# An attention stage ahead of two feed-forward stages, on one core: two-input products for scalings on VectorE, scalings shared out anew among three engines, shorter keep-warm products, and a new hand-set order with deeper rings

## The chip, the core and the metric

The kernel runs on one core of one Trainium2 chip. The metric is the device time of one execution in microseconds. Five engines of the core work side by side, each through its own queue, in the order in which the program was written: TensorE (PE; its weight loads are listed apart as PEld), VectorE (DVE), ScalarE (ACT), GpSimd (POOL) and SyncE (SP, which here only issues DMAs). An instruction that waits for another engine holds up all that stands behind it on its own engine.

## The reference

Two batches, twelve heads each, 448 positions, 64 channels per head: causal attention, then a gated feed-forward (768 to 1536 to 768) and a second one with a squared ReLU (768 to 2048 to 768). All data are float32 (the weights reach the chip as 64-bit numbers).

```python
scores = (1 / sqrt(64)) * q @ k.T            # 24 heads, 448 x 448
scores = where(above the diagonal, -1e9, scores)
attn = exp(scores - max(scores));  attn = attn / (sum(attn) + 1e-9)
x = (attn @ v), heads side by side           # 896 x 768
x = (silu(x @ w_gate) * (x @ w_val)) @ w_out
out = relu(x @ w_in2)**2 @ w_out2
```

## The kernel before

The twelve pairs of heads (p = 0 to 11; heads 2p and 2p+1) go through attention; each of the feed-forward products is made of three TensorE products of a high and a low part (`whi`, `wlo`, `ahi`, `alo`). A weight unit (128 x 768) is loaded as raw words (`wraw`) and split into `whi` and `wlo` by nine steps, J0 to J8, two on ScalarE and seven on VectorE. 68 units are split in all. Units 0 and 1 are split during attention, and unit 0 is multiplied with the first batch's result there too ("early", six steps G).

The steps of a pair, by the letters of the plan:

- LD loads q, k and v (SP). AT transposes q or k on TensorE into a bank (`qk`), AC copies it to SBUF (tile `qk`).
- S makes the scores of both heads in four row blocks i = 3, 0, 2, 1, with 448, 64, 320 and 192 columns (`s`).
- M (VectorE) scales, masks and takes the extreme value of a row, E (ScalarE) takes the exponential and its row sum, RA adds 1e-9 to four sums at a time (`guard`, tile `st`, 128x4), R is their reciprocal (VectorE).
- N scales a block of the probabilities (tile `P`) by the reciprocal: 448, 256, 192 and 64 columns; NT scales the remaining 64x64 corner. `scale_by` does both: letter D is VectorE, P is GpSimd, A is ScalarE.
- T transposes the probabilities on TensorE in two groups (`pt`): T(h, 0) waits for NT and for blocks 1 to 3 of N. H copies them to SBUF. V multiplies with v (`x`). XH copies the result (`ahi`), XL makes the rest (`alo`).

`attention_plan` lists each step with its engine, a cost, what it waits for and which ring slots it takes; `Plan.run` is a list scheduler that picks at each point the step that can start first, by rank among equals, with the table FIRST added to the ranks. The kernel is then written out in that order, so each engine's queue is fixed when the program is built. Rings set how far a step may run ahead: 8 PSUM banks, 3 raw q and k tiles (`raw`), 4 split tiles (`sp`), 6 probability tiles (`P`). While TensorE would idle in the first 24 us of the plan, `keep_warm` writes products of a constant into the next bank, each 512 columns wide.

Of the kernel before, what the change touches and what calls it, by code (L numbers as in the profile page):

```python
# [16 lines left out]
ALU = mybir.AluOpType  # L17
# [72 lines left out]
    "rings": {'bank': 8, 'raw': 3, 'rawv': 5, 'sp': 4, 'P': 6, 'pt': 4, 'wraw': 3, 'wa': 2, 'wr': 1, 'ws': 3},  # L90
    "ld0": ((1170, 2400), (520, 2450), (1050, 1900), (1050, 1950)),
    "at0": 750,
    "acd": (),
# [5 lines left out]
    "rad": (),  # L99
    "pack": 2,  # L100
    "j": (),
    "xh": (),
# [3 lines left out]
        (0, 0): 'D', (0, 1): 'D', (0, 2): 'D', (0, 3): 'D', (1, 0): 'D', (1, 1): 'D', (1, 2): 'D',  # L106
        (1, 3): 'D', (17, 2): 'D', (21, 2): 'D',
    },
    "h": {
        (17, 1): 0,  # L110
    },
    "nt": {
       
# [26 lines left out]
class Plan:  # L140
# [18 lines left out]
    def run(self):  # L159
# [16 lines left out]
        while ready:  # L176
# [19 lines left out]
            if engine == "PE":  # L196
                now = SHAPE.get(k[0])
                if shape != now:
                    cost += SWITCH[now] + 50 * (now == "columns" and not shape)
                    shape = now  # L200
                cost = warmth.run(start, cost, cols)
            free[engine] = end[k] = start + cost
            if k[0] == "J" and engine == "DVE" and k[2] in (3, 6, 7, 8):
                free["Pool"] = max(free.get("Pool", 0), start) + cost
# [26 lines left out]
def scaling(engine, n):  # L231
    return {"D": ("DVE", 135 + 0.51 * n), "P": ("Pool", max(395, 245 + 0.83 * n)),
            "A": ("ACT", 310 + 0.45 * n)}[engine]


def attention_plan(NP, NPAIR, NC, S, U, KD, rank=RANK, opt=OPT):
# [4 lines left out]
    for p in range(NP):  # L241
# [9 lines left out]
        for z in range(2):  # L251
            sp, bk = ("sp", p), ("bank", "a", p, z)
            add(("AT", p, z), "PE", 390 if p else opt["at0"], [("LD", p, z)] + ([("AT", p, 0)] if z else []), [bk] if z else [bk, sp], [raw, sp] if z else [raw], t + rank["AT"] + z / 2, cols=S * 7 / 8)
            add(("AC", p, z), *(("DVE", dve_cost(S)) if (p, z) in opt["acd"] else ("ACT", act_cost(S))), [("AT", p, z)], [], [sp, bk], t + rank["AC"] + z / 2)
# [11 lines left out]
        for h in (t, t + 1):  # L266
# [18 lines left out]
            add(("NT", h), *scaling(opt["nt"].get(h, "D"), 64), [("R", h), ("N", h, 1)], [], [P],  # L285
# [68 lines left out]
def tile_attention_moe_moe(ctx, tc, q, k, v, w_gate, w_val, w_out, w_in2, w_out2, out):  # L354
# [34 lines left out]
    def keep_warm(ps, n):  # L389
        ones = nc.const_aps.tensor(1.0, [128, 512], BF16)  # L390
        for _ in range(n):
            nc.tensor.matmul(out=ps, lhsT=ones[:, :128], rhs=ones, start=True, stop=True)
# [277 lines left out]
    def scale_by(engine, o, a, by):  # L670
        if engine == "A":
            nc.scalar.activation(out=o, in_=a, func=AF.Copy, scale=by)
        else:
# [3 lines left out]
    def normalise_tail(h):  # L677
        p, at = p_t[h], POFF[2] + 256

        scale_by(OPT["nt"].get(h, "D"), p[:64, POFF[1] + 128:POFF[1] + 192],  # L680
# [115 lines left out]
    with tc.manual_schedule():  # L796
        keep_warm(bank("idle"), 7)
        emit_consts()
        emit_fixed()
        free = 4000  # L800
# [172 lines left out]
```

## Time and profile before

| | us |
|---|---|
| runs shown: 597.0, 597.17, 596.03; median | 597.0 |
| the profiled execution's own time | 596.45 |
| its span in the trace | 594.7 |
| PE busy in the span | 582.0 (98%) |
| DVE busy | 471.4 (79%) |
| ACT busy | 280.9 (47%) |
| POOL busy | 52.5 (9%), all of it in the first 98 us |

The span is 1.75 us shorter than the execution's own time. The page's chain of the work that ended last gives 89% of the span to PE and 7% to DVE. The shares are means over stages with different limits: attention takes about the first 103 us, the feed-forward stages the rest, and POOL works in the first part alone.

### The profile page before, as it was taken

To read this page: it belongs to the slowest core of one execution; us is meant where nothing else is said; L and a number is where in the kernel's file an instruction comes from. 1 tells how busy PE (TensorE), PEld (TensorE's weight loads), DVE (VectorE), ACT (ScalarE), POOL (GpSimd) and SP (SyncE) were. 2 spreads that over 40 slices of the span, in tenths; PEclk is the share of its full clock that TensorE was granted. 3 is DMA by queue.
4 is the path that set the end of the run, shared out by engine and by line. 5 is a ranking of instruction groups with operands and counts; after the bars stand their busy time and mean duration, and the time that the engine had idled before them with its cause. 6 is when DMAs were issued, how large, how long until landed. Compare 5 with 4: busy or idle time off the path is not lost.

```text
span 594.7 us, 8720 instructions
## 1 busy us (share of the span) xinstructions
PE 582.0 (98%) x3232; PEld 531.1 (89%) x3232; DVE 471.4 (79%) x865; ACT 280.9 (47%) x532; POOL 52.5 (9%) x136
## 2 busy tenths in 40 slices
PE   9989899999999999999999999999999999999997
PEld 5756667999999999999999999999999999999997
DVE  2989987898888888888777776888888897649741
ACT  4988885443333333333333224677667733223201
POOL 2364664000000000000000000000000000000000
PEclk9999999999999999999999999999999999999999
DMA  8664231233333333333333333333333344345202
GB/s 170 146 180 104 54 122 55 94 118 106 107 107 106 107 106 109 116 117 121 114 116 107 107 107 106 107 106 107 106 107 107 106 120 147 106 147 145 69 1 93
DMA packets 80778, 65.05 MB, mean 109 GB/s; under 512 B 34912, under 2 KB 76640, under 8 KB 80736
## 3 DMA queue, kind: packets, MB, share of 16 engines
q1 hardware_dynamic: 79808, 64.27, 36.3%
q8 instruction: 25, 0.41, 0.3%
q10 hardware_dynamic: 928, 0.23, 0.2%
q14 instruction: 17, 0.14, 0.1%
HBM read 61.73 MB, written 2.75 MB: 108 GB/s over the span
## 4 chain that ended last, share of the span: by engine, by line
PE 89%; DVE 7%; issue 1%; POOL 1%; DMA 1%; SPq 0%; ACT 0%; ACTq 0%; POOLq 0%
PE o L923 20%; PE h L746 19%; PE v L746 15%; PE y L746 15%; PE g L746 14%; DVE P L642 3%; PE x L718 2%; PE s L624 2%; DVE P L674 2%; PE pt L696 1%; POOL P L674 1%; DMA raw<-in_k_dram 1%; PE early L746 1%; DVE pt L709 1%; PE qk L601 0%
## 5 line engine op out<-in xcount | busy, mean ns | idle before, releaser
L475 ACT ACTIVATE whi<-wa 128x768 fp32r<-128x768 f32 x68 | 57.4, 844 | 123.5 <-DVE wa L469 81.0
L923 PE MATMUL o<-whi,b 128*128 128x384 f32 x336 | 85.6, 334 | 0.0
L746 PE MATMUL y<-b,whi 128*128 128x480 f32 (+1 forms) x288 | 69.2, 362 | 0.0
L457 ACT ACTIVATE wa<-wraw 128x768 f32<-128x768 f32 x68 | 61.8, 909 | 11.4 <-DVE wlo L488 11.1
L746 PE MATMUL h<-b,whi 128*128 128x480 f32 (+1 forms) x256 | 66.7, 362 | 0.0
L485 DVE TENSOR_TENSOR wa<-wa,whi 128x768 f32<-128x768 f32 x68 | 64.7, 952 | 0.4 <-ACT whi L475 0.4
L482 DVE SCALAR_TENSOR_TENSOR wr<-wraw,wr 128x768 f32<-128x768 uint32 x68 | 64.8, 953 | 0.1
L488 DVE TENSOR_TENSOR wlo<-wa,wr 128x768 fp32r<-128x768 f32 x68 | 64.6, 950 | 0.2
L469 DVE SCALAR_TENSOR_TENSOR wa<-wraw,wa 128x768 uint32<-128x768 uint32 x68 | 64.6, 950 | 0.1
L460 DVE TENSOR_SCALAR wa<-wa 128x768 f32<-128x768 f32 x68 | 38.1, 561 | 32.7 <-ACT wa L457 32.7
L923 PEld LDWEIGHTS o<-whi,b 128*128 128x128 f32 x336 | 60.8, 188 | 0.0
L746 PEld LDWEIGHTS y<-b,whi 128*128 128x128 f32 x288 | 54.0, 187 | 3.6
L923 PE MATMUL o<-wlo,b 128*128 128x384 f32 x168 | 56.1, 334 | 0.0
L746 PE MATMUL h<-b,wlo 128*128 128x480 f32 x192 | 53.9, 362 | 0.0
L746 PEld LDWEIGHTS h<-b,whi 128*128 128x128 f32 x256 | 48.0, 187 | 3.2
L648 ACT ACTIVATE P<-P,st 128x320 f32<-128x320 f32 (+3 forms) x84 | 43.9, 528 | 9.5 <-DVE st L642 8.6
L642 DVE CUSTOM_DVE_ANT_0 P<-s,mask 128x448 f32<-128x448 f32 (+3 forms) x96 | 36.6, 414 | 13.3 <-issue 9.7
L833 ACT ACTIVATE b<-u 128x480 fp32r<-128x480 f32 (+2 forms) x24 | 13.9, 580 | 69.4 <-DVE u L829 69.4
L674 POOL TENSOR_SCALAR P<-P,st 128x448 f32<-128x448 f32 (+3 forms) x86 | 41.2, 494 | 18.4 <-DVE st L658 11.4
L746 PE MATMUL v<-ahi,whi 128*128 128x480 f32 (+2 forms) x144 | 40.5, 362 | 0.0
L746 PE MATMUL v<-ahi,wlo 128*128 128x480 f32 (+2 forms) x144 | 40.5, 362 | 0.0
L746 PE MATMUL v<-alo,whi 128*128 128x480 f32 (+2 forms) x144 | 40.5, 362 | 0.0
(89 smaller groups left out, 1053.4 us busy)
## 6 DMA issues: line engine op xcount, KB each, us to landing
wraw<-in_moe_w_out_dram SPq DMA_DIRECT2D x28, 768.0 KB, 4.3
wraw<-in_moe_w_in_dram SPq DMA_DIRECT2D x16, 768.0 KB, 4.7
wraw<-in_moe_w_gate_dram SPq DMA_DIRECT2D x12, 768.0 KB, 4.3
wraw<-in_moe_w_val_dram SPq DMA_DIRECT2D x12, 768.0 KB, 4.3
out_dram<-osb SPq DMA_DIRECT2D x14, 192.0 KB, 1.9
raw<-in_q_dram SPq DMA_DIRECT2D x23, 112.0 KB, 2.7
raw<-in_k_dram SPq DMA_DIRECT2D x23, 112.0 KB, 2.8
v<-in_v_dram SPq DMA_DIRECT2D x24, 96.0 KB, 2.6
```

What stands on the lines that cost most here:

```text
L457: nc.scalar.activation(out=af, in_=high.bitcast(F32), func=AF.Abs)
L460: engine.tensor_scalar(out=af, in0=af, scalar1=W_TINY, scalar2=W_HUGE, op0=ALU.max, op1=ALU.min)
L469: nc.vector.scalar_tensor_tensor(out=a, in0=high, scalar=0xC0000000, in1=a, op0=ALU.bitwise_and, op1=ALU.bitwise_or)
L475: nc.scalar.activation(out=split_t[n][0], in_=af, func=AF.Copy)
L482: nc.vector.scalar_tensor_tensor(out=rf, in0=low, scalar=2.0 ** -52, in1=rf, op0=ALU.mult, op1=ALU.mult)
L485: engine.tensor_tensor(out=af, in0=af, in1=split_t[n][0].bitcast(F32), op=ALU.subtract)
L488: engine.tensor_tensor(out=split_t[n][1], in0=af, in1=r[0].bitcast(F32), op=ALU.add)
L642: nc.vector.tensor_tensor_reduce(out=a, in0=sps.pop((h, i)), in1=mask[:rows, end - n:end], scale=-SCALE, scalar=3.0e38, op0=ALU.add, op1=A ...
L648: nc.scalar.activation(out=a, in_=a, func=AF.Exp, scale=-1.0, bias=st(0), accum_out=st(1))
L674: (nc.vector if engine == "D" else nc.gpsimd).tensor_scalar(out=o, in0=a, scalar1=by, scalar2=1.0, op0=ALU.mult, op1=ALU.mult)
L746: nc.tensor.matmul(out=pss[z][:, :cols], lhsT=w[p == 2][:, c], rhs=xs[k][p == 1][:, at:at + cols], start=first and k == 0 and p == 0, stop ...
L923: nc.tensor.matmul(out=pss[t][:, :N], lhsT=a[f][:, tk], rhs=w[:, c], start=f + n == 0, stop=f == KF2 - 1 and n == 2)
```

## The change

No step of the computation is added or left out. What the change does:

- `scale_by` has a fourth letter, B: VectorE multiplies the block with the reciprocal, read as a second input repeated along the columns (`tensor_tensor`), where letter D has a scaling by a per-partition number (`tensor_scalar`).
- N and NT: before, VectorE had 34 of the 120 scalings, all of letter D (24 NT, 2 other 64x64, 4 of 256, 2 of 448, 2 of 192 columns), GpSimd 86. Now VectorE has 4 of letter D (two of 448, one of 256, one of 192) and 29 of letter B (four of 448, six of 256, four of 192, fifteen of 64), ScalarE 16 (two of 448, two of 256, six of 192, six of 64) and GpSimd 71.
- 6 of the 24 AC copies and 4 of the 12 XH copies go from ScalarE to VectorE, 13 of the 24 RA from GpSimd to VectorE; 13 of the H copies change between ScalarE and VectorE, and VectorE still has 23.
- J7 and J8 of unit 0 go from VectorE to GpSimd, J4 of unit 1 from ScalarE to GpSimd.
- `keep_warm` counts in pieces of 128 columns. The first block stays at 7 x 512 columns. After it there were 9 x 512 = 4608 columns; now there are 256 + 512 + 512 + 128 + 384 = 1792.
- The rings `raw` and `sp` go from 3 to 4 and from 4 to 6.
- FIRST has an entry for nearly every step, and the plan's own rule for GpSimd beside VectorE is another one, so the order is new on every engine.

```diff
 FIRST = {
-    ('AC', 0, 0): 2.15, ('AC', 0, 1): 2.15, ('AC', 1, 0): 2.15, ('AC', 1, 1): 23.63,
+    ('AC', 0, 0): -4272.47, ('AC', 0, 1): -5529.96, ('AC', 1, 0): -473.91, ('AC', 1, 1): 4649.26,
...
-    "rings": {'bank': 8, 'raw': 3, 'rawv': 5, 'sp': 4, 'P': 6, 'pt': 4, 'wraw': 3, 'wa': 2, 'wr': 1, 'ws': 3},
+    "rings": {'bank': 8, 'raw': 4, 'rawv': 5, 'sp': 6, 'P': 6, 'pt': 4, 'wraw': 3, 'wa': 2, 'wr': 1, 'ws': 3},
-    "at0": 750,
-    "acd": (),
+    "at0": 700,
+    "acd": ((0, 0), (0, 1), (1, 1), (6, 1), (8, 0), (11, 1)),
-    "rad": (),
+    "rad": (0, 2, 4, 5, 9, 11, 13, 17, 18, 20, 21, 22, 23),
-    "j": (),
-    "xh": (),
+    "j": ((0, 7), (0, 8), (1, 4)),
+    "xh": (1, 2, 9, 10),
...
+            if engine == "DVE" and k[0] in ("J", "N", "NT"):
+                pool = max(free.get("Pool", 0), start)
+                if k[0] == "J" and k[2] in (1, 2, 5) or k[0] == "N" and k[1] < 2:
+                    cost += pool - start
+                    pool = start
+                free["Pool"] = pool + cost
             free[engine] = end[k] = start + cost
-            if k[0] == "J" and engine == "DVE" and k[2] in (3, 6, 7, 8):
-                free["Pool"] = max(free.get("Pool", 0), start) + cost
...
-            "A": ("ACT", 310 + 0.45 * n)}[engine]
+            "A": ("ACT", 310 + 0.45 * n), "B": ("DVE", 90 + 1.042 * n)}[engine]
...
-        for _ in range(n):
-            nc.tensor.matmul(out=ps, lhsT=ones[:, :128], rhs=ones, start=True, stop=True)
+        while n:
+            cols = min(4, n)
+            nc.tensor.matmul(
+                out=ps[:, :128 * cols], lhsT=ones[:, :128], rhs=ones[:, :128 * cols],
+                start=True, stop=True)
+            n -= cols
...
+        elif engine == "B":
+            nc.vector.tensor_tensor(out=o, in0=a, in1=by.broadcast_to(a.shape), op=ALU.mult)
...
-        scale_by(OPT["nt"].get(h, "D"), p[:64, POFF[1] + 128:POFF[1] + 192],
+        scale_by(OPT["nt"].get(h, "P"), p[:64, POFF[1] + 128:POFF[1] + 192],
...
-        keep_warm(bank("idle"), 7)
+        keep_warm(bank("idle"), 28)
-        free = 4000
+        free = 3700
-                    idle["n"] = max(0, int((start - free) / (430 if start < 6800 else 215)))
+                    idle["n"] = max(0, int((start - free) / (107 if start < 7600 else 60)))
```

How the order moves is shown at three places. The first is TensorE's queue from the third pair's scores to the first transposes of probabilities. Before:

```order
L624 MATMUL s<-qk 128x448 x2
L624 MATMUL s<-qk 128x64 x2
L624 MATMUL s<-qk 128x320 x2
L624 MATMUL s<-qk 128x192 x2
L392 LDWEIGHTS const-bfloat16-1.0
L392 MATMUL pt<-const-bfloat16-1.0 128x512
...
L689 MATMUL pt<-ident,P 128x2x64
```

After (L772 is the line of S, L537 the filling products, L839 to L849 are T, L749 is AT):

```order
L749 MATMUL qk<-ident,raw 128x112 x4
L772 MATMUL s<-qk 128x448 x2
L772 MATMUL s<-qk 128x64 x2
L537 LDWEIGHTS const-bfloat16-1.0
L537 MATMUL s<-const-bfloat16-1.0 128x512
...
L772 MATMUL s<-qk 128x320 x2
L839 MATMUL pt<-ident,P 128x2x64
L846 MATMUL pt<-ident,P 128x128 x6
L849 MATMUL pt<-ident,P 128x2x64
L772 MATMUL s<-qk 128x192 x2
```

T of head 0 now stands before the last block of the third pair's scores, and four filling products of 512 columns ahead of it have become two of 512 and one of 128.

The second place is VectorE's queue behind the second pair's XL (L734 before, L884 after). Tile P_134 is that of head 6, P_137 of head 7, P_140 of head 8. Before, with NT of heads 6, 7 and 8 (L674):

```order
L734 TENSOR_TENSOR alo1_84<-x_536,ahi1_78 128x448
L674 TENSOR_SCALAR P_134<-P_134,st_152 64x64
L709 COPY pt_583<-pt_569 128x512
L709 COPY pt_592<-pt_586 128x512
L709 COPY pt_611<-pt_605 128x512
L674 TENSOR_SCALAR P_137<-P_137,st_154 64x64
L658 RECIPROCAL st_156<-st_156 128x4
```

After, the same XL, with the two products for head 5 (L822) and the XH copy ahead of it and two AC copies (L755) behind it:

```order
L801 TENSOR_SCALAR st_162<-st_162 128x4
L806 RECIPROCAL st_162<-st_162 128x4
L822 TENSOR_TENSOR P_149<-P_149,st_162 128x192
L822 TENSOR_TENSOR P_149<-P_149,st_162 64x64
L877 CAST ahi1_78<-x_547 128x448
L884 TENSOR_TENSOR alo1_84<-x_547,ahi1_78 128x448
L755 COPY qk_503<-qk_585 128x448
L755 COPY qk_604<-qk_603 128x448
L859 COPY pt_563<-pt_595 128x512
```

NT of heads 6 and 7 has left VectorE (it stands in GpSimd's queue right behind the other blocks of its head), and other copies stand in its place.

The third place is the end of GpSimd's queue. Before, the blocks of heads 20 and 21 (P_140, P_143) and the guard between them (L653):

```order
L674 TENSOR_SCALAR P_140<-P_140,st_156 128x448
L674 TENSOR_SCALAR P_140<-P_140,st_156 128x256
L674 TENSOR_SCALAR P_140<-P_140,st_156 128x192
L674 TENSOR_SCALAR P_140<-P_140,st_156 64x64
L653 TENSOR_SCALAR st_158<-st_158 128x4
L674 TENSOR_SCALAR P_143<-P_143,st_158 128x448
```

After, with J7 and J8 of unit 0 (L633, L636) and J4 of unit 1 (L621):

```order
L824 TENSOR_SCALAR P_137<-P_137,st_154 128x256
L633 TENSOR_TENSOR wa_880<-wa_880,whi_1018 128x768
L636 TENSOR_TENSOR wlo_1019<-wa_880,wr_1092 128x768
L824 TENSOR_SCALAR P_140<-P_140,st_156 128x448
L824 TENSOR_SCALAR P_140<-P_140,st_156 128x192
L824 TENSOR_SCALAR P_140<-P_140,st_156 64x64
L621 CAST whi_1301<-wa_860 128x768
L824 TENSOR_SCALAR P_146<-P_146,st_160 128x256
```

The blocks of head 20 now wait behind two products of 768 columns.

## Rows read from the trace of the kernel before

**Rows 1.** Busy time by engine (number of instructions), two stretches in us.

```profile
24.00:91.00 67.00, 59.44 (x494) 42.85 (x492) 61.49 (x221) 57.80 (x181) 41.28 (x93) 1.00 0.44 113
103.39:594.70 491.31, 487.85 (x2527) 463.75 (x2525) 387.65 (x560) 202.06 (x298) 0.00 (x0) 1.00 0.34 107
```

**Rows 2.** Chain that ended last, in time order: start us, us, what.

```profile
8.47 3.98 PE s L624 x16
...
24.50 2.04 PE s L624 x16
...
101.50 2.05 PE early L746 x9
103.55 3.72 PE g L746 x18
107.27 7.44 PE v L746 x36
...
474.74 116.52 PE o L923 x672
```

**Rows 3.** TensorE's waits, 24 to 104 us: sum, times, longest.

```profile
PE pt L689 <- DVE P L674: 6.8, 6, 2.4
PE s L624 <- ACT qk L609: 0.8, 1, 0.8
```

**Rows 4.** Timeline of TensorE, filling products: start us, us, instruction.

```profile
15.41 1.26 PE L392 MATMUL qk<-const-bfloat16-1.0 128*128 128x512 bf16 x5
19.02 1.05 PE L392 MATMUL pt<-const-bfloat16-1.0 128*128 128x512 bf16 x4
```

**Rows 5.** Timeline of all engines, 34 to 43 us; in brackets idle before.

```profile
34.74 3.65 POOL L674 TENSOR_SCALAR P<-P,st 128x448 f32<-128x448 f32 x8 [1.18 <-PE pt L696]
...
36.27 1.76 DVE L674 TENSOR_SCALAR P<-P,st 64x64 f32<-64x64 f32 x1
...
38.09 0.33 PE L689 MATMUL pt<-ident,P 128*128 128x128 f32 x1 [2.44 <-DVE P L674]
...
42.67 0.25 DVE L674 TENSOR_SCALAR P<-P,st 64x64 f32<-64x64 f32 x1
```

**Rows 6.** Instruction groups, VectorE, to 103.4 us: busy us, mean ns | idle.

```profile
L674 DVE TENSOR_SCALAR P<-P,st 64x64 f32<-64x64 f32 x26 | 10.8, 417 | 2.0 <-POOL P L674 1.3
L734 DVE TENSOR_TENSOR alo<-x,ahi 128x448 fp32r<-128x448 f32 x12 | 7.4, 615 | 1.2 <-ACT ahi L729 1.1
L658 DVE RECIPROCAL st<-st 128x4 f32<-128x4 f32 x24 | 4.0, 172 | 1.2 <-POOL st L653 1.0
L674 DVE TENSOR_SCALAR P<-P,st 128x256 f32<-128x256 f32 x4 | 1.6, 402 | 0.0
```

**Rows 7.** VectorE's busy time, first M to last H.

```profile
10.72:99.05 88.33, 80.99 (x297) 1.00 0.47 118
```

**Rows 8.** J7 of all 68 units: shortest, median, longest in ns.

```profile
L485 DVE TENSOR_TENSOR wa<-wa,whi x68: 947/949/1111, 71.2 to 570.4; 128x768 f32<-128x768 f32 x68
```

**Rows 9.** Timeline of GpSimd, 72 to 73.6 us.

```profile
71.45 1.12 POOL L674 TENSOR_SCALAR P<-P,st 128x192 f32<-128x192 f32 x1
```

**Rows 10.** Timeline of VectorE, instructions of units 0 and 1.

```profile
71.16 1.11 DVE L485 TENSOR_TENSOR wa<-wa,whi 128x768 f32<-128x768 f32 x1
...
104.96 0.56 DVE L460 TENSOR_SCALAR wa<-wa 128x768 f32<-128x768 f32 x1 [2.21 <-ACT wa L457]
...
112.35 0.95 DVE L488 TENSOR_TENSOR wlo<-wa,wr 128x768 fp32r<-128x768 f32 x1
```

**Rows 11.** Instruction groups, GpSimd, to 103.4 us.

```profile
L674 POOL TENSOR_SCALAR P<-P,st 128x448 f32<-128x448 f32 x22 | 14.7, 669 | 15.9 <-DVE st L658 11.4 <-PE pt L696 2.2 <-PE pt L699 2.2
L674 POOL TENSOR_SCALAR P<-P,st 128x192 f32<-128x192 f32 x22 | 10.3, 470 | 0.0
```

**Rows 12.** Instruction groups, ScalarE, to 103.4 us.

```profile
L609 ACT ACTIVATE qk<-qk 128x448 f32<-128x448 f32 x24 | 12.0, 545 | 4.0 <-PE qk L601 4.0
```

**Rows 13.** DMA issues of the page: count, KB each, us to landing.

```profile
v<-in_v_dram SPq DMA_DIRECT2D x24, 96.0 KB, 2.6
```

More of the change, by code (lines that the diff above doesn't have):

```diff
@@ L105 @@
     "n": {
-        (0, 0): 'D', (0, 1): 'D', (0, 2): 'D', (0, 3): 'D', (1, 0): 'D', (1, 1): 'D', (1, 2): 'D',
-        (1, 3): 'D', (17, 2): 'D', (21, 2): 'D',
[7 rows of a table added]
     },
     "h": {
-        (17, 1): 0,
+        (2, 1): 0, (5, 0): 1, (12, 0): 1, (12, 1): 0, (15, 1): 0, (16, 0): 1, (16, 1): 0,
+        (17, 0): 1, (17, 1): 0, (18, 1): 0, (19, 0): 1, (20, 0): 1, (21, 1): 0,
     },
     "nt": {
+        3: 'B', 5: 'B', 8: 'B', 9: 'A', 12: 'B', 13: 'A', 15: 'A', 21: 'B', 23: 'B',
     },
@@ L252, in attention_plan @@
             sp, bk = ("sp", p), ("bank", "a", p, z)
-            add(("AT", p, z), "PE", 390 if p else opt["at0"], [("LD", p, z)] + ([("AT", p, 0)] if z else []), [bk] if z else [bk, sp], [raw, sp] if z else [raw], t + rank["AT"] + z / 2, cols=S * 7 / 8)
+            add(("AT", p, z), "PE", (opt["at0"], 500, 390)[min(p, 2)], [("LD", p, z)] + ([("AT", p, 0)] if z else []), [bk] if z else [bk, sp], [raw, sp] if z else [raw], t + rank["AT"] + z / 2, cols=S * 7 / 8)
             add(("AC", p, z), *(("DVE", dve_cost(S)) if (p, z) in opt["acd"] else ("ACT", act_cost(S))), [("AT", p, z)], [], [sp, bk], t + rank["AC"] + z / 2)
@@ L284, in attention_plan @@
                     [("P", h - 1), P] if packed else [P], h + rank["N"])
-            add(("NT", h), *scaling(opt["nt"].get(h, "D"), 64), [("R", h), ("N", h, 1)], [], [P],
+            add(("NT", h), *scaling(opt["nt"].get(h, "P"), 64), [("R", h), ("N", h, 1)], [], [P],
                 h + rank["N"])
```

221 rows, old and new, of tables (FIRST, OPT) are left out of this document.

## The prediction

> **What bounds the kernel now.** I read the chain of waits first. From g on [rows 2] TensorE is the whole story: the last line of the page's chain is the o products at 474.74 for 116.52 us, the span ends at 594.70, and in the 491.31 us after 103.39 TensorE is busy 487.85 [rows 1]. The change touches nothing there, except what units 0 and 1 bring along. So the end is "start of g, plus 491.15 (594.70 less 103.55), plus 1.75 outside the span", and 103.55 + 491.15 + 1.75 = 596.45, the profiled execution's own time. It lies 0.55 under the median of the runs (597.0); all sums below are on the scale of 596.45. What has to be found is the new start of g.
>
> Attention ahead of it has two engines near their limit. In 24 to 91 us TensorE is busy 59.44 of 67 us, VectorE 61.49, ScalarE 57.80, GpSimd 41.28 [rows 1]. TensorE's 7.6 us of idle time are two lines [rows 3]: 6.8 us in six waits of the transposes for VectorE's scaling (NT), the longest 2.4, and 0.8 for one copy by ScalarE. VectorE, from its first M to its last H, is busy 80.99 of 88.33 [rows 7]. Hence two floors for g, as the kernel before stands: TensorE without its waits would reach g at 103.55 − 7.6 = 95.95; VectorE without idle time would bring its last H to 10.72 + 80.99 = 91.7, and as g began 103.55 − 99.05 = 4.5 after that H, g could begin at 96.2. Whoever shortens one alone gains nothing beyond the other.
>
> Why NT is late shows in the timeline [rows 5]. GpSimd runs eight scalings from 34.74 for 3.65 us; VectorE's NT, a 64x64 corner, starts at 36.27 in the middle of them and takes 1.76 us, and TensorE has waited 2.44 when it goes on at 38.09. The same NT takes 0.25 at 42.67. So the mean of 417 ns [rows 6] holds stalls beside GpSimd, and a stalled NT holds up all that is queued on VectorE behind it.
>
> **The filling products.** TensorE's granted clock is 1.00 in both stretches [rows 1], yet the first 16 score products take 3.98 us at 8.47 and the same 16 take 2.04 at 24.50 [rows 2]: half rate at first, the lower of its two levels, 1.2 GHz, and 2.4 later. The nine filling products behind the first block take 1.26 + 1.05 = 2.31 us [rows 4], 0.50 ns a column. The new 1792 columns would take 0.90, a gain of 1.4. What could be lost is the clock: if fewer fillers let the second pair's scores run at half rate too, they cost 3.98 in place of 2.04, that is +1.9. I take −1.4, since other products now stand in those gaps, and keep −1.4 to +0.5 for the range.
>
> **VectorE's work.** Gone: 24 NT and 2 like them, 26 x 0.417 = 10.8; four blocks of 256 at 0.402, 1.6 of which one stays, and the two of 448 and one of 192 that stay too, so 1.2; J7 and J8 of unit 0 at 0.949 [rows 8], 1.9. Sum 13.9. Come: the 29 products of two inputs. A line through 0.615 at 448 columns [rows 6] and 0.949 at 768 [rows 8] has 1.04 ns a column and gives 0.415 at 256, 0.348 at 192, 0.214 at 64: 4 x 0.615 + 6 x 0.415 + 4 x 0.348 + 15 x 0.214 = 9.6. Ten copies come, priced as that 448-column row, 0.615; three AC copies belong to the start, before the first M, one XH is behind the last H, so six count: 3.7. Thirteen guards come, priced like the reciprocal of the same 128x4 at 0.172 [rows 6]: 2.2. The last XL goes behind the last H: −0.6. Net −13.9 + 15.5 − 0.6 = +1.0; about as much overlaps at the starts of successive short instructions, so I put VectorE's sum as unchanged within 1 us. VectorE is not relieved. What it loses is the stretched instructions; what it must lose for a gain is its idle time. By its floor, with the half microsecond of gain or loss that I can't settle, the last H ends near 91.1 to 91.7. Behind it TensorE had 4.5 us (V of the last pairs, then the early products 101.50 to 103.55 [rows 2]); the new order goes from V11 straight to g, as the six G steps stand between the T steps, so 2.45 remain: g at 93.6 to 94.2.
>
> **TensorE's waits.** Without any, and with the fillers' 1.4, g starts at 103.55 − 7.6 − 1.4 = 94.55, just above VectorE's floor. So the bound is TensorE's order and how well the other three engines keep up. The 0.8 for the q and k copy goes with the deeper rings and the copies that VectorE takes over; the 2.4 is a stall that can't recur in this form, as NT is now mostly in GpSimd's own queue. Of the other 4.4 I leave 60%, 2.6 us, since a new order always leaves some transposes waiting; ends 0 and 7.6. Gain 5.0, and 6.4 with the fillers.
>
> **What is hidden.** ScalarE takes 16 scalings, each no dearer than the 0.545 of its 448-column copy [rows 12]: at most 8.7, and gives away ten such copies, 5.5, and one cast. At most +3 on 57.80 of 67 in the tightest stretch; its cover is 9.2 us there. GpSimd loses 15 scalings and 13 guards and gets three J steps; it waited 15.9 us ahead of its 448-column blocks [rows 11]. SP's queue now has the last loads of v behind W0 and W1 and a v load behind the slot of an earlier V: 2.6 us to landing [rows 13], with the ATs, three T groups and the last scores (about 5.4 us) on TensorE ahead of its use; free.
>
> J7 and J8 on GpSimd stand ahead of head 20's blocks. No row has a product of two inputs there. Below: GpSimd's slope from 0.470 at 192 to 0.669 at 448 [rows 11], 0.78 ns a column, gives 0.92 at 768. Above: twice that, 1.84, and 1.2 for being held by VectorE, 3.0. By VectorE's sum J6 ends some 15.8 us before g, and T(20, 0) stands 10.35 before it: 5.4 us, of which head 20's blocks need 1.5, so up to 1.95 each is free and at 3.0 they cost 2.1. I take 1.84 and nothing. A page alone has this very operation: the Trainium skill, "GPSIMD Engine Reference", section "2.1 Instruction dispatch", puts two-input elementwise work at some 2.5 cycles an element, an estimate of 1.6 us here, and no run yet shows it; by it the cost is nothing too.
>
> Unit 1's split runs beside g and v: before, from 104.96 to 113.30 (112.35 and 0.95 [rows 10]), and o's unit is needed at g + 3.72 + 7.44 = 11.2 [rows 2]. In the new order VectorE reaches it about 1.5 us after g starts: 1.5 + 8.3 = 9.8. It has 1.3 to spare.
>
> **The sum.** 596.45 − 1.4 − 5.0 = 590.05; **590.0**, g at 97.1. On the median's scale that would be 590.6.
>
> **The rivals.** *All waits go*: g at 94.55, **587.4**. For it: the planner has a new rule for GpSimd beside VectorE and every step is placed anew. Against: ScalarE has 9 us of slack only, and three engines feed each transpose.
>
> *VectorE keeps its 7.3 us of idle time* (88.33 − 80.99), because its order waits for R and M as before: last H at 98.4 as by rows 7, less what the fillers give; 98.4 + 2.45 = 100.9 for g, **593.8**. For it: its sum is unchanged. Against: much of the idle time is of the kind that the stall brought about.
>
> *The products are held by GpSimd as NT was.* J7 shows 1.111 at 71.16 where the median is 0.949 [rows 8, 10], and at 71.45 a GpSimd scaling of 192 columns takes 1.12 [rows 9] in place of 0.470 [rows 11]. So the two hold each other: GpSimd lost 0.65 and VectorE 0.16. If VectorE loses 0.16 at each of 29 products, 4.7, then 93.6 + 4.7 + the 2.6 of waits is 100.9, again **593.8**. The trace speaks for a mild form: the side that started first lost little. The Trainium skill, "SBUF — State Buffer", section "SBUF: two separate sides", speaks against the change more strictly: a VectorE operation with two SBUF inputs takes the port pair that it shares with GpSimd as an exclusive lock against a GpSimd operation that reads SBUF, and the loser blocks fully. By that rule the swap of a scaling for a product frees VectorE from nothing; by the row above it loses a sixth of a microsecond at worst, and the loss is GpSimd's.
>
> *GpSimd becomes the last of each head (slower).* NT of 15 heads stands behind the other blocks in GpSimd's queue. By the slope above a 64-column scaling is 0.37; 29 products that each hold GpSimd for their mean of 0.33 are 9.6 us, 0.40 a head. If the transposes of those 15 heads wait for it, 15 x 0.77 = 11.6 us of waits replace the 7.6: 103.55 − 7.6 − 1.4 + 11.6 = 106.2, **599.1**. It decides from (7.6 + 1.4) / 15 = 0.60 a head on. For it: the corner is now the last piece of a queue whose other pieces the transposes need as well. Against: none of TensorE's waits was ended by GpSimd [rows 3], and it had 15.9 us of idle time to be earlier [rows 11].
>
> **How the numbers follow.** Forecast 0.47; all waits go 0.15; idle time stays 0.13; products held 0.12; GpSimd last 0.13. The forecast's own range, with waits from 1.5 to 5 and the fillers' and J's doubt, is 588.5 to 592.5. To leave out no more than 2 in 10 (the last rival, and what lies below the first) the range is 586.0 to 595.5. About 1.2 us, 0.2%, is what a measurement of this kernel can tell from no change. Of the cases four are faster by more; I give 0.05 to two of them coming together and 0.02 of the last to "no change": faster 0.82, same 0.07, slower 0.11.
>
> **What would show it.** Right: g starts within a microsecond of 97; TensorE's idle time in 24 to 91 is 2 to 4 us and VectorE's NT no longer ends it; no 64-column scaling on VectorE over 0.5; the second pair's scores at 2.0. Wrong: products far over 0.615 at 448 columns (the lock); transposes that wait for GpSimd, above all T(20, 0) behind J7 and J8 (over 1.95 each); scores at 3.98 twice (the clock); o waiting for unit 1; an unchanged 7 us of idle time on VectorE. My weakest number is the 2.6 us of waits left in an order whose times no trace has shown.

## The result, and the profile after

The changed kernel takes 589.3 us (median of four runs, 589.21 to 592.0), the kernel before 596.64 (596.03 to 597.17) beside it: a ratio of 0.9888, with a 95% interval of 0.9858 to 0.9918. The time forecast was 590.0, its range 586.0 to 595.5. The profiled execution took 589.21 us, its span is 587.3.

The end of the chain that ended last, in order of time (start us, us, what), answers to [rows 2]:

```profile
7.72 1.17 PE s L772 x8
...
76.78 2.06 DVE wr L630
...
92.39 3.61 PE x L868 x32
96.00 3.90 PE g L896 x18
99.90 7.44 PE v L896 x36
...
467.37 116.52 PE o L1073 x672
```

g starts at 96.00 instead of 103.55, and from there to the end of the span it is 491.3 us, as it was 491.15: the whole gain is made ahead of g. The early products now stand earlier, so that g follows V directly.

TensorE's waits from 24 to 97 us (us in total, times, longest) answer to [rows 3]:

```profile
PE pt L839 <- DVE P L822: 0.8, 2, 0.5
PE pt L839 <- POOL P L824: 0.5, 1, 0.5
PE pt L849 <- ACT P L820: 0.5, 1, 0.5
PE x L868 <- ACT pt L861: 0.3, 1, 0.3
PE pt L839 <- ACT P L820: 0.2, 1, 0.2
```

7.6 us of waits have become 2.3, shared among three engines, none over 0.5.

Busy time by engine (number of instructions) from VectorE's first M to the end of its last H, first of before, then of after; the second line of after is 24 us to g:

```profile
10.72:99.13 88.41, 80.56 (x649) 59.29 (x648) 81.07 (x297) 74.79 (x228) 48.98 (x110) 1.00 0.47 118
```

```profile
8.98:93.11 84.13, 81.20 (x642) 59.39 (x640) 80.99 (x312) 76.61 (x237) 42.80 (x85) 1.00 0.48 119
24.00:96.00 72.00, 69.68 (x566) 51.66 (x562) 69.66 (x250) 62.87 (x191) 38.07 (x74) 1.00 0.45 116
```

The third figure is VectorE: 81.07 us of work before, 80.99 after, the same sum, in a stretch that is 4.3 us shorter (88.41 to 84.13). What it lost is idle time, 7.3 to 3.1. By the timelines the start of g moved by 7.46 (103.39 to 95.93), in three parts: the first M comes 1.74 earlier, the stretch is 4.28 shorter, and from the last H to g it is 2.82 where it was 4.26, so 1.44. The stretch from the first M to the last H is the measure for the experiments too; the way from the first M to g, which leaves out the start as well, is 92.67 us before and 86.95 after, 5.7 less.

### The profile page after: what moved, and what is told of

The parts are those of the page before. It is cut to its first block, busy times and chain, and to the rows that moved or that the text cites. A ratio compares the mean times of both kernels' runs of the same rounds, so it can differ in the third digit from the quotient of the medians.

```text
span 587.3 us, 8681 instructions
## 1 busy us (share of the span) xinstructions
PE 579.2 (99%) x3228; PEld 528.6 (90%) x3228; DVE 474.7 (81%) x885; ACT 280.4 (48%) x537; POOL 46.3 (8%) x111
## 4 chain that ended last, share of the span: by engine, by line
PE 87%; DVE 10%; ACT 1%; issue 1%; DMA 1%; SPq 0%; POOL 0%; POOLq 0%; ACTq 0%
PE o L1073 20%; PE h L896 20%; PE v L896 15%; PE y L896 15%; PE g L896 14%; DVE P L790 5%; DVE pt L859 1%; PE s L772 1%; DVE P L822 1%; PE x L868 1%; PE pt L846 1%; DMA raw<-in_k_dram 1%; DVE alo L884 1%; ACT P L796 0%; SPq L728 0%
## 5 line engine op out<-in xcount | busy, mean ns | idle before, releaser
L633 DVE TENSOR_TENSOR wa<-wa,whi 128x768 f32<-128x768 f32 x67 | 63.7, 951 | 0.4 <-ACT whi L623 0.4
L636 DVE TENSOR_TENSOR wlo<-wa,wr 128x768 fp32r<-128x768 f32 x67 | 63.7, 951 | 0.1
L796 ACT ACTIVATE P<-P,st 128x448 f32<-128x448 f32 (+3 forms) x84 | 43.9, 526 | 5.3 <-DVE st L790 3.2
L896 PE MATMUL y<-b,wlo 128*128 128x480 f32 (+1 forms) x144 | 40.4, 362 | 0.0
L626 DVE TENSOR_SCALAR wr<-wa 128x768 uint32<-128x768 uint32 x68 | 38.0, 559 | 1.8
```

Source lines behind the costliest of these rows:

```text
L626: nc.vector.tensor_scalar(out=r[0], in0=a, scalar1=0xFF800000, scalar2=None, op0=ALU.bitwise_and)
L633: engine.tensor_tensor(out=af, in0=af, in1=split_t[n][0].bitcast(F32), op=ALU.subtract)
L636: engine.tensor_tensor(out=split_t[n][1], in0=af, in1=r[0].bitcast(F32), op=ALU.add)
L796: nc.scalar.activation(out=a, in_=a, func=AF.Exp, scale=-1.0, bias=st(0), accum_out=st(1))
L896: nc.tensor.matmul(out=pss[z][:, :cols], lhsT=w[p == 2][:, c], rhs=xs[k][p == 1][:, at:at + cols], start=first and k == 0 and p == 0, stop ...
```

## The experiments

Ten of the twelve kernels keep the order of the steps of one of the two kernels and change what stands at some places of it; the last two change the order. The median of the kernel before beside them was between 596.47 and 596.61.

**Products back to scalings.** In the changed kernel:

```diff
-            nc.vector.tensor_tensor(out=o, in0=a, in1=by.broadcast_to(a.shape), op=ALU.mult)
+            nc.vector.tensor_scalar(out=o, in0=a, scalar1=by, scalar2=1.0, op0=ALU.mult, op1=ALU.mult)
```

> The changed kernel with one line undone: the 29 two-input products on VectorE are one-input scalings again, each in the same place of the same queues. Theory (a product loses little beside GpSimd, a scaling is stretched by it): undisturbed scalings would be 1.7 us shorter in all (0.45, 0.35, 0.32 and 0.25 us by width, in place of 0.64, 0.42, 0.35 and 0.28), but stretched ones add some 0.2 us each; VectorE was busy 81.0 of 84.1 us between its first M and its last H, so nearly all of it reaches the end: 591 to 594 us. Rival (products are held by GpSimd just as scalings are): VectorE only gains the 1.7 us: 587.5 to 589.3. Rival (VectorE's order alone matters, not these operations): 589.3 within 0.6.

590.04 us (589.34 to 591.54, four runs), not to be told from the changed kernel's 589.3. The 64-column scalings took 288 ns on average where the products take 276, so at these places hardly anything stretches either form. By the stretch, 84.94 us for 84.13, the kind of operation is worth less than 1 us in the new order; four runs of each can't show so little. My 0.2 us of stretch each did not come.

**Scalings to products, in the kernel before.** All 34 scalings of letter D, nothing else.

```diff
+        elif engine == "D":
+            nc.vector.tensor_tensor(out=o, in0=a, in1=by.broadcast_to(a.shape), op=ALU.mult)
```

> The kernel before with one part of the change alone: all 34 scalings on VectorE become two-input products; the order is untouched. Theory (stretched NT are what TensorE waits for): 26 corners of 64 columns go from a mean of 0.417 to some 0.28 us, and the 1.76 and 1.61 us stalls go: TensorE's waits of 6.8 us shrink by 3 to 4: 592.5 to 594 us. Rival (the order and the shared-out work made the gain): the waits stay, 596 to 597.2. Rival (products are held like scalings): 596.5 to 598.

596.51 us (eleven runs), a ratio of 1.0003 (0.9992 to 1.0014). The theory fell. The timelines of VectorE, GpSimd and TensorE at the place of [rows 5] (start us, us, instruction; in brackets the idle time before it):

```profile
34.54 1.79 DVE L674 TENSOR_TENSOR P<-P,st 64x64 f32<-64x64 f32 x1
```

```profile
33.63 3.04 POOL L676 TENSOR_SCALAR P<-P,st 128x256 f32<-128x256 f32 x7
```

```profile
36.39 0.33 PE L691 MATMUL pt<-ident,P 128*128 128x128 f32 x1 [2.44 <-DVE P L674]
36.55 1.42 PE L698 MATMUL pt<-ident,P 128*128 128x128 f32 x6
```

A product of 64 columns takes 1.79 us beside GpSimd's run of scalings, where the scaling took 1.76, and 0.21 alone: it is held to the full. The other places are the same too: 0.94, 1.64 and 0.63 us for the products where the scalings took 0.94, 1.61 and 0.59. TensorE waits the same 2.44.

**What GpSimd holds.** Work that nothing reads, on GpSimd beside the feed-forward stages:

```diff
+        for _ in range(90):
+            nc.gpsimd.tensor_scalar(
+                out=side, in0=side, scalar1=0.5, scalar2=1.0, op0=ALU.mult, op1=ALU.mult)
+        for _ in range(54):
+            nc.gpsimd.tensor_tensor(out=side, in0=side, in1=side, op=ALU.mult)
+        for _ in range(150):
+            nc.gpsimd.memset(side, 0.0)
```

> The changed kernel with idle work on GpSimd behind attention, beside the feed-forward stages, on a tile that nothing reads: 90 scalings of 128x448, then 54 products of the tile with itself, then 150 memsets, back to back. VectorE's steps J there have a usual time each (J7 and J8, two inputs, 0.95 us; J1, J2, J5, one input, 0.56; J3 and J6, 0.95 to 0.97). If two-input steps are held fully by a running scaling of 0.67 us, J7 and J8 grow by 0.3 to 0.7 us each in the first stretch; if they only share, by some 0.16 us as the one row of before showed. Beside the memsets both expect the usual times. The time itself is slower where VectorE then holds up TensorE.

631.68 us in one run. Groups of instructions (busy us, mean ns | idle), first 110 to 150 us, beside the scalings, then 300 to 340 us, beside the memsets:

```profile
L634 DVE TENSOR_TENSOR wa<-wa,whi 128x768 f32<-128x768 f32 x5 | 5.4, 1086 | 0.0
L614 DVE TENSOR_SCALAR wa<-wa 128x768 uint32<-128x768 uint32 x5 | 4.6, 915 | 0.0
L988 DVE TENSOR_TENSOR u<-v,sg 128x480 f32<-128x480 f32 x2 | 1.3, 638 | 0.0
L995 DVE TENSOR_TENSOR b<-u,b 128x480 fp32r<-128x480 f32 x1 | 1.0, 1005 | 0.0
L963 POOL TENSOR_SCALAR side<-side 128x448 f32<-128x448 f32 x38 | 37.7, 992 | 3.1
```

```profile
L634 DVE TENSOR_TENSOR wa<-wa,whi 128x768 f32<-128x768 f32 x6 | 5.7, 944 | 0.0
L614 DVE TENSOR_SCALAR wa<-wa 128x768 uint32<-128x768 uint32 x6 | 3.4, 572 | 0.0
L988 DVE TENSOR_TENSOR u<-v,sg 128x480 f32<-128x480 f32 x1 | 0.7, 657 | 1.6 <-PE v L897 1.6
L995 DVE TENSOR_TENSOR b<-u,b 128x480 fp32r<-128x480 f32 x1 | 0.7, 652 | 0.0
L968 POOL MEMSET side<- 128x448 f32 x67 | 36.4, 543 | 3.9
```

Beside scalings J7 grows from 0.94 to 1.09 us, the product b of two SBUF tiles from 0.65 to 1.00, the one-input J2 from 0.57 to 0.92; the product u, one of whose inputs (v) lies in PSUM, stays at 0.64. GpSimd's own scaling grows from 0.67 [rows 11] to 0.99. Beside GpSimd's products of 1.3 us J7 took 1.49 (235 to 260 us). Beside memsets the two-input steps are as usual. So two-input products from SBUF are held by a GpSimd operation that reads SBUF, and hold it in turn, as one-input scalings are and do; the product with an input in PSUM is free of it. How far they are held differs: J7's 0.14 us beside scalings is the size that I had given for sharing, its 0.55 beside GpSimd's products that for holding.

**NT on GpSimd, in the kernel before.** One letter:

```diff
-        scale_by(OPT["nt"].get(h, "D"), p[:64, POFF[1] + 128:POFF[1] + 192],
+        scale_by(OPT["nt"].get(h, "P"), p[:64, POFF[1] + 128:POFF[1] + 192],
```

> The kernel before with NT of all 24 heads on GpSimd instead of VectorE, nothing else. VectorE loses 10 us of work and every stall of NT; GpSimd gains 24 x 0.34 = 8 us, and each head's first transposes now wait for GpSimd's last block. Theory (VectorE's time and idle time set the pace): 592 to 595. Rival (GpSimd becomes the last of each head): 598 to 603, with TensorE's waits ended by GpSimd.

590.7 us (589.93 to 592.29), a ratio of 0.9913 (0.9897 to 0.9929): below the theory's 592, and four fifths of the whole change's gain by the medians, in the old order. The two intervals overlap. By the way from the first M to g, 88.66 us, it is 4.0 of the 5.7 us. Its busy times from the first M to the last H, and TensorE's wait:

```profile
10.47:94.86 84.39, 79.78 (x649) 58.07 (x648) 70.73 (x273) 74.28 (x228) 55.96 (x134) 1.00 0.50 125
```

```profile
PE pt L689 <- POOL P L674: 4.6, 4, 1.5
```

VectorE's work falls from 81.07 to 70.73 us and the stretch from 88.41 to 84.39, nearly that of the changed kernel (84.13). GpSimd does become the last of a head, in four waits of 4.6 us together; that is less than the 6.8 that went. VectorE's idle time grows from 7.3 to 13.7 us, so it no longer sets the pace there.

**The same, with work put back on VectorE.** A reciprocal of a tile of its own at each place where NT stood.

```diff
+        nc.vector.reciprocal(out=side, in_=side)
```

> The kernel before with NT on GpSimd, as in the run of 590.7 us, and at each place where NT stood in VectorE's queue a reciprocal of 128x256 ones on a tile of its own, some 0.35 us, that waits for nobody and nobody waits for it; so VectorE has 24 x 0.35 = 8.4 of the 10.8 us back. Theory (VectorE's amount of work sets the pace): 594 to 596.5. Rival (what counts is that VectorE is held at these places and TensorE waits for it, not how much it does): 590 to 592.

616.99 us. The reciprocal took 1.74 us, not 0.35, so five times as much work came back as I meant: VectorE is busy 107.33 us in a stretch of 110.67. So the dose was missed. The kernel shows that VectorE's amount of work sets the pace once it is the longest, with idle time of 3.3 us left, but not where between 70.7 and 107.3 us it begins to. Whether the old order loses by VectorE's work or by the stalls stays open.

**NT back on VectorE, in the changed kernel.** The reverse letter for the 15 heads.

```diff
-        scale_by(OPT["nt"].get(h, "P"), p[:64, POFF[1] + 128:POFF[1] + 192],
+        scale_by(OPT["nt"].get(h, "D"), p[:64, POFF[1] + 128:POFF[1] + 192],
```

> The changed kernel with NT of the 15 heads that GpSimd has taken over back on VectorE, as one-input scalings like before; every other row of every queue stays. Theory (what the change gains is that these corners no longer stand in VectorE's queue, where they wait for GpSimd's port use and hold up the rest): VectorE, busy 81.0 of 84.1 us, gets 15 x 0.42 = 6 us more: 593 to 596. Rival (the new order and the fillers made the gain, not where NT stands): 589 to 590.5, with TensorE's waits below 4 us.

594.59 us (593.5 to 596.44, twelve runs). The stretch from the first M to the last H, and TensorE's waits for these scalings:

```profile
9.05:97.80 88.75, 81.80 (x642) 58.70 (x640) 84.92 (x327) 77.19 (x237) 37.98 (x70) 1.00 0.46 113
```

```profile
PE pt L839 <- DVE P L824: 3.6, 5, 1.9
```

The stretch is 88.75 us, VectorE busy 84.92. The 15 scalings take 4.3 us, 285 ns each: they are hardly stretched there, and the stretch grows by 4.6 all the same. So in the new order what costs is not a stall beside GpSimd but the work added to VectorE's queue, 3.9 us by its busy time, and the transposes wait for it.

**Products given to GpSimd, in the changed kernel.**

```diff
-            nc.vector.tensor_tensor(out=o, in0=a, in1=by.broadcast_to(a.shape), op=ALU.mult)
+            nc.gpsimd.tensor_scalar(out=o, in0=a, scalar1=by, scalar2=1.0, op0=ALU.mult, op1=ALU.mult)
```

> The changed kernel with the 29 products that VectorE makes given to GpSimd as one-input scalings, each at its place in the plan's order. VectorE loses 10.6 us of 81.0; GpSimd, busy 42.8 of 84.1, gets 4 x 0.68 + 6 x 0.59 + 4 x 0.56 + 15 x 0.34 = 13.6 us. Theory (VectorE sets the pace, GpSimd has room): 587 to 588.7, as TensorE has only 2 to 3 us of waits left to lose. Rival (the products stand on VectorE because GpSimd would be the last of those heads): 590 to 595, with TensorE's waits ended by GpSimd.

591.19 us (589.9 to 591.27). VectorE's work falls from 80.99 to 73.04 us, and the stretch is 84.74, not shorter. TensorE now waits for GpSimd:

```profile
PE pt L839 <- POOL P L824: 1.2, 2, 1.0
PE pt L839 <- POOL P L822: 1.1, 3, 0.6
PE pt L846 <- POOL P L824: 0.4, 2, 0.3
```

So near 84 us the stretch is held by more than one engine: 4 us more on VectorE cost 4.6, 8 us less, put on GpSimd, give nothing. The theory fell.

**J7 and J8 of unit 0 back on VectorE, in the changed kernel.**

```diff
-        engine = nc.gpsimd if early else nc.vector
+        engine = nc.gpsimd if early and n else nc.vector
```

> The changed kernel with J7 and J8 of unit 0 on VectorE again; all queues else as they are. In the trace J6 of unit 0 took 2.15 us beside J7 on GpSimd, where 0.95 is usual: the move cost VectorE 1.2 us and saved it 1.9. Theory (VectorE's sum is the path): 589.3 + 0.7 = 590.0, between 589.3 and 591. Rival (GpSimd's 3.6 us for J7 and J8 hold up head 20's blocks, and these the transposes): 586.5 to 588.7.

589.66 us (589.48 to 590.82): no difference that four runs can tell. What the move saves VectorE it gives back in good part, since J6 of unit 0 on VectorE is held by J7 on GpSimd. The timelines of the changed kernel:

```profile
76.20 1.82 POOL L633 TENSOR_TENSOR wa<-wa,whi 128x768 f32<-128x768 f32 x1
```

```profile
76.69 2.15 DVE L630 SCALAR_TENSOR_TENSOR wr<-wraw,wr 128x768 f32<-128x768 uint32 x1
```

J6 starts 0.49 us into J7, ends 0.82 us after it, and takes 2.15 where 0.95 is usual; in the run with J7 and J8 on VectorE it takes 0.95. The chain runs through it.

**The filling products, each way.** The new count in the kernel before (below), and the reverse in the changed kernel.

```diff
-        for _ in range(n):
-            nc.tensor.matmul(out=ps, lhsT=ones[:, :128], rhs=ones, start=True, stop=True)
+        while n:
+            cols = min(4, n)
...
-                    idle["n"] = max(0, int((start - free) / (430 if start < 6800 else 215)))
+                    idle["n"] = max(0, int((start - free) / (107 if start < 7600 else 60)))
```

> The kernel before with the new filling products alone: by the new count its plan leaves 256 columns ahead of the last k transposes of the first pair, and 2304 + 1792 where it had 2560 + 2048. The columns saved are 0.25 us. Theory (the fillers' worth is small where VectorE holds TensorE up later): 595.8 to 596.8. Rival (the piece of 256 columns lets the clock rise before the first scores, and the 2 us reach the end): 594 to 595.

596.61 us, a ratio of 0.9998 (0.9988 to 1.0008).

> The changed kernel with the old filling products: three of 512 columns behind the first block in place of 256 + 512 + 512 + 128 + 384, none ahead of the last k transposes of the first pair. Theory (the new order, not the count, took the fillers away, and the clock's rise at the start comes at another moment from one execution to the next): 589.0 to 590.3, and the first scores at either rate. Rival (the 256 columns make the early rise): the first 16 scores take 4.0 us and the time is 591 to 592.5.

590.86 us (589.24 to 591.94, five runs); the profiled execution took 589.24, with the first 16 scores in 2.11 us, without any filler ahead of them, and its stretch at 84.19. The old count leaves 1536 columns in the new order, fewer than the new count's 1792. So the new order, not the pieces of 128, took the fillers away. The two counts differ by 512 columns behind the first block in the old order and by 256 in the new, and neither difference is worth anything that these runs can tell.

**The order and the rings.** The changed kernel with the rings of before, and, in the first of the two, the table FIRST of before as well:

```diff
-    "rings": {'bank': 8, 'raw': 4, 'rawv': 5, 'sp': 6, 'P': 6, 'pt': 4, 'wraw': 3, 'wa': 2, 'wr': 1, 'ws': 3},
+    "rings": {'bank': 8, 'raw': 3, 'rawv': 5, 'sp': 4, 'P': 6, 'pt': 4, 'wraw': 3, 'wa': 2, 'wr': 1, 'ws': 3},
```

> The changed kernel with the table FIRST and the two rings of before: who does what, the products, the fillers and the planner's rule are new, the hand-set order is not; the planner makes the order out of the rest. Theory (moving NT off VectorE is the bulk): 590 to 592.5. Rival (without its table the shared-out work fits badly, and the order is part of the gain): 593.5 to 600.

596.9 us, a ratio of 1.0009 (0.9999 to 1.0019): the gain is gone. Its stretch:

```profile
9.09:101.29 92.20, 84.89 (x658) 61.14 (x655) 82.62 (x313) 76.48 (x236) 42.00 (x85) 0.96 0.46 117
```

Part of it is the clock: between 54 and 69 us TensorE is idle for 5.4 us, 3.0 of them in one wait for GpSimd, and its granted clock there is 0.81. It is busy 84.89 us, where it is 81.20 in the changed kernel.

> The changed kernel with rings raw 3 and sp 4 as before, FIRST as changed; the order differs at few places. Theory (deeper rings are worth at most the 0.8 us wait for a q or k copy): 589.3 to 590.3. Rival (the new order needs the depth): 591.5 to 595.

595.86 us, a ratio of 0.9986 (0.9974 to 0.9997): nearly all of it is gone. TensorE's idle time in it, from its timeline:

```profile
58.84 0.33 PE L839 MATMUL pt<-ident,P 128*128 128x128 f32 x1 [1.50 <-POOL P L824]
...
74.76 0.33 PE L839 MATMUL pt<-ident,P 128*128 128x128 f32 x1 [1.90 <-POOL P L824]
```

The theory of each fell, and the rivals came about, the second a little beyond its range. With the short rings the planner places the transposes of q and k from about the seventh pair on elsewhere, scalings and splits follow in another order, and GpSimd gets a run of nine scalings of 6.49 us (55.23 to 61.72); the stretch is 88.23 and 5.7 us pass from the last H to g. The table of the new order is made for the deep rings. That the depth alone would help the old table was not tried, so what the rings are worth by themselves stays open.

## Why the prediction came out right, and where its reasons were not

**Right in the measure.** The forecast split the gain into 5.0 us of TensorE's waits and 1.4 us of fillers. The waits went from 7.6 to 2.3, so 5.3; I had left 2.6. g came at 96.00, where 97.1 was forecast; with a first M at 10.72 as before it would have come at some 97.7, by my estimate (95.93 and 1.74). VectorE's sum was put as unchanged within 1 us and came out at 80.99 for 81.07. The products cost 0.644, 0.421, 0.349 and 0.276 us where the line through two rows gave 0.615, 0.415, 0.348 and 0.214. J7 and J8 took 1.82 and 1.81 us on GpSimd for 1.84, and head 20's blocks behind them waited another 0.85 us, for VectorE. (The Trainium skill, "GPSIMD Engine Reference", section "2.1 Instruction dispatch", led to an estimate of 1.6; the trace differs by an eighth, and decides.) From the last H to g 2.45 us were forecast, 2.82 measured. Unit 1's split held nobody up: 491.3 us from g to the end of the span.

**The fillers' term was wrong.** Its 1.4 us showed in neither run on the count, though these changed it by far less than the 2816 columns that the change takes away, and that removal was not run by itself. In the kernel before VectorE is busy 12.53 of the 13.28 us from its first M to 24 us, so there the fillers, which all stand in that time, can have held it up by 0.75 us at most by then: I took TensorE's time off where VectorE had next to none to gain. By the profiled executions something else stands in the place of the 1.4: the first 16 score products, 3.98 us in [rows 2], take 2.11 us at 7.65 in the changed kernel, the higher of TensorE's two levels, and the first M comes 1.74 us earlier. But that is no work of the change. Four kernels share the queue of the kernel before up to there, and their first M came at 10.72 (before), 10.47 (NT on GpSimd), 9.10 (products) and 8.99 us (reciprocals). Among those with the changed kernel's queue it came at 8.95 to 9.05 in three (the changed kernel itself, NT back, the GpSimd work) and at 10.09 to 10.46 in four (scalings, J7 and J8 back, products on GpSimd, old rings). The clock rises at another moment from one execution to the next. So of the 7.46 us between the two profiles 5.7 belong to the change (4.28 and 1.44), and the rest to two starts that happened to differ; that the medians differ by 7.3 with an interval of about 4.9 to 8.5 us fits both. The forecast's total is nearer to the median than its terms are to the truth.

**What brought the 5.0 was half understood.** I wrote that VectorE is not relieved, and that the stall at NT is the thing that goes. NT leaving VectorE's queue is indeed enough for 4.0 of the 5.7 us from the first M to g. But the stall was less than half of TensorE's waits in the kernel before. Of the six in [rows 3] two, 2.44 and 0.75 us, ended on a stretched NT (1.76 and 1.61 us). The other four, 3.6 us together, ended on one of 0.25 us, which came late in VectorE's queue; two of them, NT and the transpose that waits for it:

```profile
66.64 0.25 DVE L674 TENSOR_SCALAR P<-P,st 64x64 f32<-64x64 f32 x1
66.95 0.33 PE L689 MATMUL pt<-ident,P 128*128 128x128 f32 x1 [1.09 <-DVE P L674]
...
75.32 0.25 DVE L674 TENSOR_SCALAR P<-P,st 64x64 f32<-64x64 f32 x1
75.63 0.33 PE L689 MATMUL pt<-ident,P 128*128 128x128 f32 x1 [1.16 <-DVE P L674]
```

Whether an earlier stall or VectorE's amount of work made these late is not shown. The run with NT back in the new order shows that plain work counts there (4.3 us of work, 4.6 us of stretch), where hardly one is stalled. The change moves 10 us off VectorE and puts as much on it again: products, copies, guards. In the order that the planner makes from the old table that filling up costs everything (596.9), and the new order with its deep rings wins it back and a little more. Against NT on GpSimd alone the rest of the change shortens the stretch by 0.26 us (84.39 to 84.13) and the way from the last H to g by 1.45. Which of the moved pieces costs the 6.2 us between 590.7 and 596.9 was not tried one by one.

**The deep rings.** I gave them the 0.8 us wait for a copy. Without them the new table loses nearly all of the gain (595.86), since the planner then makes another order of it.

**The products and GpSimd.** From J7's 1.11 us [rows 8, 10] I took a loss of a sixth of a microsecond at worst for VectorE. That was the step that misread its row: in that one meeting GpSimd's scaling was the one held most (1.12 us for 0.470), and I took what VectorE lost there for its worst case. A product of 64 columns took 1.79 us in the kernel with products alone. The Trainium skill, "SBUF — State Buffer", section "SBUF: two separate sides", had it right: a VectorE operation with two SBUF inputs and a GpSimd operation that reads SBUF exclude each other, and the loser blocks fully. The runs agree on who holds whom, down to the memsets, beside which J7 kept its 0.944 us; the 1.79 us, beside seven scalings that took 3.04 together, lasted for several of them. This did not cost the forecast its rival's 593.8, as in the new order the products are seldom held (the 15 of 64 columns take 0.276 on average).

**The rivals.** That all waits go would have put g at 94.55; it came to 95.93 with an early clock. That VectorE keeps its idle time did not happen with the full change (3.1 us), but does with the old table and rings (92.20 less 82.62, 9.6 us). That GpSimd becomes the last of a head is real in the kernel with NT there alone (4.6 us in four waits), with the products there (2.7), with the old rings (3.4) and with the old table (3.0), but for a few heads and not for each, and none of these is slower than the kernel before.

## What to carry to other kernels

An instruction that is held by another engine, or stands late in a full queue, holds up the engine that waits for it; moving it into the queue of the engine that holds it took 5.8 us off here with one letter, where changing its form took nothing. Once two engines are within some 3 us of the stretch, as TensorE and VectorE are here at 84 us, moving work from one of them to a third gave nothing and loading one cost in full. The planner's new table was worth next to nothing without the ring depths that it was made for. And before a term of 1 to 2 us is credited to an edit, look whether the unchanged start differs between the two profiles.

## What the runs showed of the hardware that was not expected

**A two-input product is held like a scaling.** VectorE's products from SBUF and GpSimd's operations that read SBUF hold each other (1.79 for 0.21 us; J7 1.09 beside scalings and 1.49 beside GpSimd's products, for 0.94); with one input in PSUM they do not (0.64 and 0.66). Some one-input steps over SBUF are held by memsets as well: J1 and J5, of some 0.56 us, took 0.73 and 0.81 beside them, J2 its usual 0.57.

**The clock at the start, and after a wait.** The first score products run at the lower or the higher level in executions with the same queue ahead of them, and the granted clock of 4 to 14 us does not tell which: it is 1.00 for 3.98 and for 2.11 us, and 0.66 for the 4.00 us of the kernel with scalings. In the kernel with products alone TensorE reached the long wait 1.7 us earlier than in the kernel before, waited the same 2.44 us, and then ran at half rate: its next six transposes took 1.42 us for 0.82, and the granted clock of that stretch is 0.76, in the third figure from the end:

```profile
34.00:41.00 7.00, 4.61 (x22) 3.54 (x24) 4.48 (x7) 4.62 (x14) 4.38 (x12) 0.76 0.71 185
```

By 45 us its lead was 0.1 us. The kernel before, after the same wait, went on at full rate.

**Reciprocal is slow by the column.** 128x256 took 1.74 us, 128x4 took 0.17: 6.2 ns a column, six times the product's 1.04.
